# Attention before a feed-forward block: whose work the first pass's exponentials and block sums are

## The chip, the cores and the metric

The kernel runs on one core of a Trainium2 chip. The metric is the device time of one execution in microseconds (us). The core's engines work side by side, each through its own queue in order: TensorE (PE, with its weight loads PEld), VectorE (DVE), ScalarE (ACT), GpSimd (POOL) and SyncE (SP), which here only issues DMAs.

## The reference

```python
# q, k, v: (8, 8, 576, 64), float32
k_p = k.reshape(B, H, 72, 8, D).mean(axis=3)          # 72 keys: means of 8 neighbours
v_p = v.reshape(B, H, 72, 8, D).mean(axis=3)
scores = scale * np.matmul(q, k_p.transpose(0, 1, 3, 2))
scores = scores - np.max(scores, axis=-1, keepdims=True)
attn = np.exp(scores)
attn = attn / (np.sum(attn, axis=-1, keepdims=True) + 1e-09)
x = np.matmul(attn, v_p)                                # -> (4608, 512), heads side by side
gate = 1.0 / (1.0 + np.exp(-(x @ w_gate)))              # w_gate, w_val: (512, 1536)
return gate * (x @ w_val) @ w_out                       # w_out: (1536, 512)
```

## The kernel before

The 4608 rows of x are cut into nine blocks j of 512 (NB = 9, BT = 512). The weights come as 64-bit floats and are turned into float32 on the chip by bit work on ScalarE and VectorE (`to_f32`, steps "conv" and "oconv"). Each operand of a large product is split into a rounded part and a rest, so a product is three matmuls (h·h, h·l, l·h).

There are two parts. The **first pass** (`first_pass`) does attention for blocks 0, 1 and 2, converts all weights, does the whole feed-forward block for block 0 and stores it. After it, a loop of four rounds treats two blocks each with a fast scheme of seven products in place of eight (`hidden_second`, `hidden`, `second_sums`), while attention of later blocks is done piece by piece in between (`attention`).

In the first pass the steps for a block j, a pair of heads p (four pairs) and a half hf of the 512 queries are, by the names used below:

- `keys` sums eight neighbours of k on VectorE into 72 keys; `put` scales them and puts them into a block-diagonal tile `kbd` (ScalarE, two instructions of 64x72). There are five such tiles, kbd_88 to kbd_92, used in turn.
- `sc` gives the scores in PSUM: 128 queries x 4 groups x 72 keys, so 288 a row. `max` takes the negated maximum of each group of 72.
- `exps` makes the exponential. Before, it is four ScalarE instructions of 72 scores each, with the negated maximum as bias.
- `sum` adds each row's exponentials, `main` and `rest` divide by the sums, `turn` and `rturn` transpose on TensorE, `hi`/`lo` split the result, `av` multiplies by the values, `x`/`xl` split the product into the operands (tiles `xo`) of the feed-forward block.
- `vsum` and `rsum` sum eight neighbours of v for blocks 1 and 2 on VectorE (the 64 main keys, and the 8 others); block 0's are made by TensorE (`pv`).
- `mm` are the products with w_gate and w_val (tiles `chain`), `gate` and `h` join them, `acc` is the product with w_out.

In the profile the names of the first pass's scratch tiles are short: `early` is a large tile in which keys, maxima, sums and the exponentials of pairs 2 and 3 lie; `e` holds the exponentials of pairs 0 and 1; `raw`, `raws` and part of `early` are where q, k and v land.

Three tables of numbers set the order. `ORDER` lists the first pass's steps in the order in which buffers are given; it is the same in both kernels. `UNREAD` says how many matmuls whose result nobody reads are put ahead of a step (`bank_for` issues them); they are 128x128 matmuls of a constant tile. `LATER` is a permutation of all recorded instructions of the whole program, from which each engine's queue follows; semaphores between engines come from the data. All engine calls are recorded through one helper, so that nearly every row of the profile has one line, L319; tiles tell the steps apart.

Of the kernel before, what the change touches and what calls it, by code (L numbers as in the profile page):

```python
# [61 lines left out]
    "sc.0.1.1": 10, "sc.0.1.0": 1, "sc.0.0.1": 1, "sc.0.2.0": 5, "sc.0.3.1": 7, "sc.0.3.0": 2, "sc.1.0.0": 1,  # L62
    "rturn.0.1": 5, "av.0.3": 1, "mm.0.0": 1, "mm.0.1": 5, "mm.1.0": 2, "mm.1.1": 1, "mm.0.2": 1, "sc.1.1.0": 1,
# [268 lines left out]
def attention_then_ffn(ctx: ExitStack, tc: tile.TileContext, qT, kT, vm, vr, vn, sums8, wgv, wo, const, out, outT):  # L332
# [759 lines left out]
    def first_pass():  # L1092
# [79 lines left out]
        def keys(j, p):  # L1172
            k = raws["k", j, p] if j else got[f"k{p}"].rearrange("p (g t) -> p g t", t=POOL)
            nc.vector.reduce_sum(out=ks[j, p][:, :KEYS], in_=k, axis=AX.X)
# [87 lines left out]
        def v_sum(j, p):  # L1262
            pool(vs[j, p], raws["v", j, p], nc.vector)
# [199 lines left out]
```

## Time and profile before

| what | value |
|---|---|
| median of 3 runs | 934.22 us (932.6 to 936.99) |
| the profiled execution's own time | 933.27 us |
| its span, first to last instruction | 931.5 us |
| granted TensorE clock, mean | 0.999 |
| busy: PE / DVE / ACT / POOL | 918.0 / 695.0 / 572.4 / 24.1 us |
| instructions: PE / DVE / ACT / POOL | 4375 / 1062 / 1044 / 59 |
| DMA | 223.13 MB, mean 240 GB/s |

An engine's busy time says how long it had an instruction under way; matmuls overlap, so a busy PE need not run at its full pace. A fp32 matmul that is not split (scores, the unread ones) leaves two records, so 4375 records are 4159 matmuls. The views used are: the page's totals, a table of stretches of the span, the groups of like instructions, the timeline, and the chain of work that ended last.

### The profile page before, as it was taken

What the parts mean: (1) busy time and instruction counts of PE and PEld (TensorE: products, weight loads), DVE (VectorE), ACT (ScalarE), POOL (GpSimd) and SP (SyncE); (2) the same over time, 40 slices, a digit from 0 to 9 for tenths busy, and PEclk for the clock granted to TensorE, in tenths of its full rate; (3) what the DMA queues carried; (4) which work ended last, traced back from release to release, by engine and by line L of the source; (5) the groups of instructions that cost most, each with busy time, mean ns of one, the idle gap of its engine ahead of it and who ended that gap; (6) DMA issues with size and microseconds to landing.
All of it is one profiled execution on the core that took longest, in us unless ns stands there. A gap on an engine that the chain in (4) does not pass through costs nothing.

```text
span 931.5 us, 12557 instructions
## 1 busy us (share of the span) xinstructions
PE 918.0 (99%) x4375; PEld 756.0 (81%) x4375; DVE 695.0 (75%) x1062; ACT 572.4 (61%) x1044; POOL 24.1 (3%) x59
## 2 busy tenths in 40 slices
PE   8999999999999999999999999999999999999998
PEld 7778788887888878888888888888888878888886
DVE  6998888899999997976789956464768573544763
ACT  7999998679989764665575636443554353234442
POOL 1000000011121000000000000000000000000000
PEclk9999999999999999999999999999999999999999
DMA  9999496778889757787667567545456675566266
GB/s 341 372 354 346 164 392 226 254 264 304 289 303 340 265 192 262 265 301 243 210 212 235 191 223 232 191 166 186 156 193 203 216 235 191 177 198 191 94 212 192
DMA packets 90367, 223.13 MB, mean 240 GB/s; under 512 B 9536, under 2 KB 28480, under 8 KB 88768
## 3 DMA queue, kind: packets, MB, share of 16 engines
q1 hardware_dynamic: 85184, 203.97, 64.9%
q0 software_dynamic: 5120, 18.35, 5.1%
q8 instruction: 35, 0.57, 0.2%
q14 instruction: 28, 0.23, 0.1%
HBM read 168.81 MB, written 53.48 MB: 239 GB/s over the span
## 4 chain that ended last, share of the span: by engine, by line
PE 92%; ACT 5%; DMA 2%; DVE 1%; issue 0%; POOL 0%; ACTq 0%; POOLq 0%
PE chain L319 54%; PE acc L319 27%; PE sc L319 4%; PE av L319 4%; PE tp L319 2%; ACT e L319 1%; DMA parts<-keptV0C 1%; DMA oparts<-keptS 1%; ACT w L319 1%; ACT L319 1%; DMA oparts<-keptO 0%; ACT raw L319 0%; ACT y L319 0%; PE vp L319 0%; ACT parts L319 0%
## 5 line engine op out<-in xcount | busy, mean ns | idle before, releaser
L319 PE MATMUL chain<-xo,parts 128*128 128x512 f32 x2316 | 558.6, 394 | 2.9 <-ACT y L319 1.4
L319 PEld LDWEIGHTS chain<-xo,parts 128*128 128x128 f32 x2316 | 427.2, 188 | 93.4 <-ACT y L319 2.1
L319 PE MATMUL acc<-hs,oparts 128*128 128x512 f32 (+1 forms) x1011 | 235.3, 390 | 0.8 <-DMA oparts<-keptO 0.5
L319 PEld LDWEIGHTS acc<-hs,oparts 128*128 128x128 f32 x1011 | 188.2, 188 | 41.6 <-issue 1.4
L319 DVE TENSOR_TENSOR hs<-h,hs 128x1024 fp32r<-128x1024 f32 x52 | 63.3, 1221 | 37.9 <-ACT hs L319 37.5
L319 ACT CAST hs<-h 128x1024 fp32r<-128x1024 f32 x52 | 54.6, 1053 | 52.6 <-PE acc L319 51.4
L319 DVE TENSOR_TENSOR y<-chain,sG 128x512 f32<-128x512 f32 x69 | 47.2, 686 | 45.6 <-PE chain L319 32.3
L319 DVE TENSOR_TENSOR y<-chain,sV 128x512 f32<-128x512 f32 x69 | 47.2, 686 | 37.3 <-PE chain L319 25.8
L319 ACT COPY sV<-chain 128x512 f32<-128x512 f32 x69 | 40.3, 586 | 52.4 <-PE chain L319 48.6
L319 ACT COPY sG<-chain 128x512 f32<-128x512 f32 x69 | 40.4, 586 | 48.3 <-PE chain L319 47.7
L319 ACT ACTIVATE gate<-y 128x512 f32<-128x512 f32 x69 | 43.2, 631 | 39.7 <-DVE y L319 35.2
L319 ACT CAST hs<-s 128x1024 fp32r<-128x1024 f32 x36 | 37.9, 1054 | 39.8 <-PE acc L319 24.2
L319 ACT ACT_TABLE_LOAD x47 | 60.3, 1283 | 1.4 <-DVE y L319 0.5
L319 DVE TENSOR_TENSOR hs<-s,hs 128x1024 fp32r<-128x1024 f32 x36 | 44.0, 1221 | 14.6 <-ACT hs L319 14.4
L319 DVE TENSOR_TENSOR h<-y,gate 128x512 f32<-128x512 f32 x69 | 47.4, 689 | 3.8 <-ACT gate L319 1.8
L319 PE MATMUL sc<-kbd,raw 128*128 128x144 f32 (+1 forms) x260 | 41.0, 295 | 1.0 <-ACT other L319 0.7
L319 PEld LDWEIGHTS sc<-kbd,raw 128*128 128x128 f32 (+1 forms) x260 | 33.5, 177 | 9.8 <-issue 2.8
L319 PE MATMUL acc<-oparts,hs 128*128 128x512 f32 x144 | 37.8, 399 | 0.1
L319 DVE TENSOR_REDUCE m<-sc 128x4 f32<-128x288 f32 x48 | 21.7, 452 | 14.3 <-PE sc L319 14.0
L319 PEld LDWEIGHTS acc<-oparts,hs 128*128 128x128 f32 x144 | 26.3, 188 | 5.5 <-ACT pr L319 0.3
L319 DVE TENSOR_TENSOR h<-h 128x256 f32<-128x256 f32 (+2 forms) x39 | 28.3, 728 | 0.7
L319 ACT ACTIVATE gate<-chain 128x512 f32<-128x512 f32 x23 | 13.8, 599 | 18.9 <-PE chain L319 18.5
(193 smaller groups left out, 1026.0 us busy)
## 6 DMA issues: line engine op xcount, KB each, us to landing
oparts<-keptS SPq DMA_DIRECT2D x48, 512.0 KB, 4.1
oparts<-keptO SPq DMA_DIRECT2D x72, 256.0 KB, 3.5
raw<-in_wgv SPq DMA_DIRECT2D x12, 1024.0 KB, 8.7
out<-o SPq DMA_DIRECT2D x35, 256.0 KB, 4.4
raw<-in_kT SPq DMA_DIRECT2D x28, 288.0 KB, 4.8
raw<-in_qT SPq DMA_DIRECT2D x29, 256.0 KB, 4.4
raw_o<-in_wo SPq DMA_DIRECT2D x12, 512.0 KB, 6.7
keptO<-oparts SPq DMA_DIRECT2D x12, 512.0 KB, 3.8
```

Of the source, the lines that this page charges most:

```text
L319: return self._book.take(lambda: f(*args, **named))
```

## The change

`exps` becomes two instructions: VectorE adds the negated maxima to all 288 scores of a half, from PSUM into the tile of exponentials in SBUF, and ScalarE makes one exponential of the 288 in place. For blocks 1 and 2 the sums of keys and values and the scaling in `put` go to GpSimd. On GpSimd a sum is three additions, of 4, 2 and 1 columns per group (`pool`, which is there before and was given VectorE until now). Block 0's key sums stay on VectorE and its `put` on ScalarE.

```diff
 UNREAD = {
-    "sc.0.1.1": 10, "sc.0.1.0": 1, "sc.0.0.1": 1, "sc.0.2.0": 5, "sc.0.3.1": 7, "sc.0.3.0": 2, "sc.1.0.0": 1,
...
+    "sc.0.1.1": 3, "sc.0.1.0": 2, "sc.0.0.1": 5, "sc.0.0.0": 3, "sc.0.2.1": 2, "sc.0.2.0": 2, "sc.0.3.1": 2,
...
 LATER = """
-2 17 15 11 34 5 10 35 19 14 6 36 12 8 3 37 18 4 7 38 16 9 39 13 28 40 41 20 42 43 24 46 58 90 25 91 92 23 26 93 94 79
...
         def keys(j, p):
             k = raws["k", j, p] if j else got[f"k{p}"].rearrange("p (g t) -> p g t", t=POOL)
-            nc.vector.reduce_sum(out=ks[j, p][:, :KEYS], in_=k, axis=AX.X)
+            pool(ks[j, p][:, :KEYS], k, nc.gpsimd if j else nc.vector)
 
         def place_keys(j, p):
             t = kbd[slot(j, p)]
             for r, c in ((slice(0, D), slice(0, KEYS)), (slice(D, P), slice(KEYS, 2 * KEYS))):
-                nc.scalar.activation(t[r, c], ks[j, p][r, :KEYS], AF.Copy, scale=SCALE)
+                if j:
+                    nc.gpsimd.tensor_scalar(out=t[r, c], in0=ks[j, p][r, :KEYS], scalar1=SCALE, scalar2=None, op0=ALU.mult)
+                else:
+                    nc.scalar.activation(t[r, c], ks[j, p][r, :KEYS], AF.Copy, scale=SCALE)
 
         def exps(j, p, hf):
             v = scs[j, p, hf].rearrange("p i (h k) -> p (i h) k", h=2)
-            for i in range(QT):
-                k = QT * hf + i
-                nc.scalar.activation(es[p // 2][:, p % 2, k], v[:, i], AF.Exp, bias=maxima[j, p][:, k:k + 1])
+            k = slice(QT * hf, QT * hf + QT)
+            e = es[p // 2][:, p % 2, k]
+            nc.vector.tensor_tensor(
+                out=e, in0=v, in1=maxima[j, p][:, k, None].broadcast_to([P, QT, KEYS]), op=ALU.add,
+            )
+            nc.scalar.activation(e, e, AF.Exp)
...
         def v_sum(j, p):
-            pool(vs[j, p], raws["v", j, p], nc.vector)
+            pool(vs[j, p], raws["v", j, p], nc.gpsimd if j else nc.vector)
...
         def r_sum(j, g):
-            pool(vsr[j, g][:96], raws["r", j, g], nc.vector)
+            pool(vsr[j, g][:96], raws["r", j, g], nc.gpsimd if j else nc.vector)
```

`UNREAD` comes to 44 unread matmuls before and 47 now. `LATER` is another permutation from its first number to its last, so the order differs over the whole program. Three places follow. In them `early<-h` is a sum of block 0's keys, `early<-sc` with 128x4 a maximum, `zs` the row sums of exponentials, `pm` and `rest` what is divided by them, `w_235` the first weight tile under conversion.

VectorE at the start, before:

```order
L319 TENSOR_REDUCE early<-h 128x72 x2
L319 TENSOR_REDUCE early<-sc 128x4 x2
L319 TENSOR_REDUCE early<-h 128x72
L319 TENSOR_REDUCE early<-sc 128x4 x2
L319 TENSOR_REDUCE early<-h 128x72
L319 TENSOR_REDUCE early<-raw 128x64
L319 TENSOR_REDUCE early<-sc 128x4
L319 TENSOR_REDUCE zs<-e 128x16
```

VectorE at the start, now:

```order
L320 TENSOR_REDUCE early<-h 128x72 x3
L320 TENSOR_REDUCE early<-sc 128x4
L320 TENSOR_TENSOR early<-sc,early 128x288
L320 TENSOR_REDUCE early<-sc 128x4
L320 TENSOR_TENSOR early<-sc,early 128x288
L320 TENSOR_REDUCE early<-sc 128x4 x2
L320 TENSOR_TENSOR e<-sc,early 128x288
L320 TENSOR_REDUCE early<-sc 128x4
L320 TENSOR_TENSOR e<-sc,early 128x288
L320 TENSOR_REDUCE early<-sc 128x4
L320 TENSOR_TENSOR e<-sc,early 128x288 x2
L320 TENSOR_REDUCE early<-sc 128x4
```

All four key sums of block 0 (the first and a small cast stand just ahead of these rows) now come before the first maximum, and six halves have their maxima and additions before the first row sums (`zs<-e`, the next row); before, five maxima and a value sum of block 1 stood there.

GpSimd, where the clearing of tiles ends, before:

```order
L319 MEMSET vl_102 128x128
L319 MEMSET vh_95 128x128
L319 MEMSET vl_99 128x128
L319 DMA keptG4A<-parts 128x1024
L319 DMA keptG4B<-parts 128x1024
```

GpSimd in the middle of its new work, around the `put` of block 1's pair 2 into kbd_89, now:

```order
L320 TENSOR_TENSOR raw_217<-raw_217 128x72x4
L320 TENSOR_TENSOR early_200<-raw_216 128x72
L320 TENSOR_TENSOR raw_217<-raw_217 128x72x2
L320 TENSOR_TENSOR early_200<-raw_217 128x72
L320 TENSOR_TENSOR raws_210<-raws_210 96x64x2
L320 TENSOR_TENSOR early_200<-raws_210 96x64
L320 TENSOR_TENSOR raw_218<-raw_218 128x72x4
L320 TENSOR_SCALAR kbd1_89<-early_200 64x72 x2
```

Before, nothing stood between the clearing and the DMAs of the later loop; now 60 additions and 16 scalings do (20 sums and 8 `put`s). Eleven sums and the first addition of a twelfth, `keys.2.3` (raw_218), stand ahead of that `put`.

TensorE at the scores of that pair, before:

```order
L319 MATMUL chain<-xo_263,parts 128x512 x12
L319 MATMUL sc<-kbd_89,early 128x144 x2
L319 MATMUL sc<-kbd_90,early 64x144
L319 MATMUL sc<-kbd_89,early 64x144
L319 MATMUL sc<-kbd_89,early 128x144
L319 MATMUL chain<-xo_263,parts 128x512 x9
```

TensorE there, now:

```order
L320 MATMUL chain<-xo_253,parts 128x512 x3
L320 MATMUL sc<-kbd_90,early 64x144
L320 MATMUL sc<-kbd_89,early 64x144
L320 MATMUL sc<-kbd_89,early 128x144
L320 MATMUL chain<-xo_253,parts 128x512 x3
```

The scores from kbd_89 now wait for GpSimd where they waited for ScalarE, and products of the feed-forward block stand behind them in TensorE's queue in both.

More of the change, by code (lines that the diff above doesn't have):

```diff
@@ L61 @@
 UNREAD = {
-    "sc.0.1.1": 10, "sc.0.1.0": 1, "sc.0.0.1": 1, "sc.0.2.0": 5, "sc.0.3.1": 7, "sc.0.3.0": 2, "sc.1.0.0": 1,
-    "rturn.0.1": 5, "av.0.3": 1, "mm.0.0": 1, "mm.0.1": 5, "mm.1.0": 2, "mm.1.1": 1, "mm.0.2": 1, "sc.1.1.0": 1,
[4 rows of a table added]
 }
```

307 rows, old and new, of tables (LATER, UNREAD) are left out of this document.

## Prediction

> **What bounds the kernel now.** I read the page's totals and its chain first, then the stretches, then the groups and the timeline of the first 55 us.
>
> ```profile
> PE 918.0 (99%) x4375; PEld 756.0 (81%) x4375; DVE 695.0 (75%) x1062; ACT 572.4 (61%) x1044; POOL 24.1 (3%) x59
> PE 92%; ACT 5%; DMA 2%; DVE 1%; issue 0%; POOL 0%; ACTq 0%; POOLq 0%
> 767.60 101.10 PE chain L319 x444
> ```
>
> TensorE is busy for 99% of the span and carries 92% of the chain, so only what lets it run denser can shorten the kernel. Its full pace is read from the longest piece of the chain: 444 matmuls of 512 columns in 101.10 us, 0.2277 us each. I gave each matmul the usual distance from its start to the next one's, form by form (0.227 us for the 512-wide). The matmuls that are read come to 889 us of the span's 931.5; the 44 unread ones come to 10, and about 28 us is waiting. That work cannot shrink, so the most that any change here can win is some 38 us, and much of that is start-up. The stretches (us busy, count in brackets, then granted clock, DMA share and GB/s) say where it lies:
>
> ```profile
> 0.00:13.50 13.50, 10.79 (x72) 10.41 (x72) 5.63 (x12) 7.01 (x26) 2.48 (x19) 1.00 0.87 320
> 13.50:37.00 23.50, 21.40 (x128) 17.11 (x129) 22.34 (x45) 21.54 (x59) 0.00 (x0) 1.00 1.04 371
> 37.00:100.00 63.00, 61.69 (x304) 49.56 (x303) 59.73 (x99) 60.26 (x120) 0.00 (x0) 1.00 0.91 330
> 100.00:175.00 75.00, 73.88 (x363) 60.50 (x362) 61.24 (x99) 64.31 (x119) 1.74 (x3) 1.00 0.70 265
> 175.00:330.00 155.00, 153.63 (x748) 126.05 (x747) 148.76 (x258) 132.33 (x273) 19.86 (x37) 1.00 0.84 290
> 330.00:700.00 370.00, 369.99 (x1772) 305.62 (x1771) 269.09 (x415) 197.84 (x332) 0.00 (x0) 1.00 0.65 217
> 700.00:928.00 228.00, 226.62 (x1000) 186.71 (x998) 127.77 (x140) 89.02 (x120) 0.00 (x0) 1.00 0.60 192
> ```
>
> By the same account TensorE is behind its full pace (time less read work done) by 10.6 us at 13.5, 18.3 at 37, 22.1 at 69, 22.6 at 100, 26.4 at 175, 31.8 at 330, 37.1 at 700 and 38.6 at the end. So half of the loss falls in the first 37 us and 13 of the rest by 330. There VectorE (third pair of numbers) and ScalarE (fourth) are full too: 95 and 92% in the second stretch, 95 and 96% in the third, VectorE 96% in 175 to 330. After 330 neither is. The change touches the right stretch: it must be weighed by VectorE's and ScalarE's queues there, not by their sums over the span.
>
> **ScalarE, removed and added.** All rows of groups below are of the first 260 us.
>
> ```profile
> L319 ACT ACTIVATE early<-sc,early 128x72 f32<-128x72 f32 x48 | 12.4, 325 | 0.6 <-DVE early L319 0.5
> L319 ACT ACTIVATE e<-sc,early 128x72 f32<-128x72 f32 x48 | 12.3, 324 | 3.4 <-DVE early L319 3.4
> L319 ACT ACTIVATE kbd<-early 64x72 f32<-64x72 f32 x24 | 6.3, 263 | 2.5 <-DVE early L319 2.3
> L319 ACT CAST r<-rest 128x256 fp32r<-128x256 f32 x8 | 3.3, 409 | 3.1 <-DVE rest L319 3.1
> L319 ACT CAST parts<-w 128x512 fp32r<-128x512 f32 x24 | 14.7, 631 | 0.9 <-DVE w L319 0.5 <-PE chain L319 0.3
> ```
>
> 96 exponentials of 72 go: 24.7 us. 16 of the 24 `put` instructions go: 16 x 0.263 = 4.2. 24 of 288 come; no row has one, but 256 columns took 409 ns and 512 took 631, so 437 by a straight line: 10.5. ScalarE loses 18.4 us of work (17 to 19 by the two rows as ends). It is then no longer last before 175 us. I count this at nothing in the sum, since VectorE stands just as full beside it; it is the cover that lets the other terms act, and up to 4 us more if ScalarE caused the 3.8 us that TensorE falls behind between 100 and 175.
>
> **VectorE, removed and added.**
>
> ```profile
> L319 DVE TENSOR_REDUCE early<-raw 128x72 f32<-128x576 f32 x8 | 5.9, 742 | 0.0
> L319 DVE TENSOR_REDUCE early<-raws 128x64 f32<-128x512 f32 x4 | 2.7, 678 | 0.0
> L319 DVE TENSOR_REDUCE early<-raws 96x64 f32<-96x512 f32 x4 | 2.6, 672 | 0.0
> L319 DVE TENSOR_REDUCE early<-raw 128x64 f32<-128x512 f32 x3 | 2.0, 675 | 0.0
> L319 DVE TENSOR_REDUCE early<-early 128x64 f32<-128x512 f32 x1 | 0.7, 667 | 0.0
> L319 DVE TENSOR_REDUCE early<-sc 128x4 f32<-128x288 f32 x24 | 10.6, 451 | 4.8 <-PE sc L319 4.7
> L319 DVE TENSOR_TENSOR h<-h 128x256 f32<-128x256 f32 x16 | 6.8, 422 | 0.4
> L319 DVE TENSOR_TENSOR h<-h 128x512 f32<-128x512 f32 x8 | 5.5, 685 | 0.1
> ```
>
> The 20 sums of blocks 1 and 2 go: 5.9 + 2.7 + 2.6 + 2.0 + 0.7 = 13.9 us. 24 additions of 288 come, at 455 ns between the 422 and 685 of 256 and 512 columns, which is what a maximum over the same 288 takes (451): 10.9. **First term: -3.0 us** (ends -3.8 at 422 and 0 at 580).
>
> The second term is VectorE's idle time at the start:
>
> ```profile
> 3.45 1.53 DVE L319 TENSOR_REDUCE early<-h 128x72 f32<-128x576 f32 x2 [2.58 <-DMA h<-in_kT]
> 8.48 0.95 DVE L319 TENSOR_REDUCE early<-sc 128x4 f32<-128x288 f32 x2 [3.50 <-PE sc L319]
> 12.73 0.46 DVE L319 TENSOR_REDUCE early<-sc 128x4 f32<-128x288 f32 x1 [0.63 <-PE sc L319]
> 13.48 1.35 DVE L319 TENSOR_REDUCE zs<-e 128x16 f32<-128x1152 f32 x1 [0.29 <-ACT e L319]
> ```
>
> Up to the first row sums at 13.48 it waits 7.0 us in four waits, and has done 5.6 us of work. Now the four key sums (3.0 us) come first; the last one's keys are the seventh of the DMAs, 1.8 MB, there near 7 us at the 371 GB/s of the second stretch and a start of 2. They end near 8. From there each half brings a maximum and an addition, 0.9 us, while TensorE gives a half in 0.6, so VectorE waits no more; six additions and seven maxima later the row sums start at about 13.3, with 8.3 us done. **Second term: -2.9 us** (ends 0 and -3.5: the waits of 3.50 + 0.63 + 0.29 less what the later landing adds).
>
> **GpSimd** takes 60 additions and 16 scalings. Nothing in the trace adds on GpSimd; the nearest rows are its clearings:
>
> ```profile
> L319 POOL MEMSET kbd<- 128x144 f32 x5 | 1.0, 221 | 0.3 <-POOLq L1454 0.3
> L319 POOL MEMSET vh<- 128x128 f32 x5 | 1.0, 205 | 0.0
> L1454 POOL MEMSET const-float32-0.0<- 128x1 f32 x1 | 0.1, 98 | 0.2 <-issue 0.2
> ```
>
> That is 0.10 us and 0.85 ns a column: 0.34 + 0.22 + 0.16 = 0.72 us a sum, 14.5 for all, and 2.6 for the scalings: 17 us as the lower end. An addition reads twice what a clearing writes; three times, 51 us, is my upper end. I take twice, 34 us (the clearing's rate, once for each operand). It hides as long as it comes before its reader. The tightest place is `put` 1.2 for the scores here:
>
> ```profile
> 53.90 1.47 PE L319 MATMUL sc<-kbd,early 128*128 128x144 f32 x9
> ```
>
> Ahead of it stand eleven sums and one addition; the twelfth's keys are the 48th DMA, 16.5 MB into the queue. By 37 us 13.0 MB are there (13.5 x 320 + 23.5 x 371 kB), and at 330 to 371 GB/s the rest takes 9.3 to 10.5: 46 to 48 us. The scores now stand 2.3 us of work earlier in TensorE's queue than at 53.90, and run at 50 to 52. So GpSimd has some 3 us to spare, and its own work (eleven sums of 1.4 in the 30 us since the first values landed) fits. Taken at nothing.
>
> **Three more unread matmuls**, 0.22 us each: they stand where TensorE waits, but I charge 0.7 (ends 0 and 0.7). The DMAs are the same; the order past 330 us differs, and I count that at 0 (ends -2 and +2, half of what TensorE falls behind from 330 to 700).
>
> **The sum**: -3.0 - 2.9 + 0.7 = -5.2 on the profiled execution's 933.27 (span 931.5 and 1.8 around it), 928.1. The median of the runs is 0.95 above that execution, so 929.0 us.
>
> **Rivals.** (1) *It stays within 0.5%, because VectorE's queue keeps the deadline.* TensorE's first products need the splits of x, the last of which is here:
>
> ```profile
> 36.55 1.28 DVE L319 TENSOR_TENSOR xo<-av,xo 128x512 fp32r<-128x512 f32 x2
> ```
>
> Ahead of the second one stood 27.9 us of VectorE's work by the groups' durations, and now 29.4: eight additions came in, two sums went out. With 2.9 us less idle time that is only 1.4 us earlier; the sums it is spared lie later, when VectorE is 96% busy in 175 to 330 with work that waits for TensorE's results. Then the gain is 1.4 and the time 933. For it: that stretch is full. Against it: between 37 and 100 VectorE is spared most sums, and TensorE lost 4.3 us there.
>
> (2) *Slower: GpSimd's additions hold up VectorE.* If the two block each other while both read SBUF, VectorE loses GpSimd's time in the share of its own that is open to it. Its costliest such rows from 13.5 to 100 us:
>
> ```profile
> L319 DVE TENSOR_TENSOR parts<-w,parts 128x512 fp32r<-128x512 f32 x17 | 11.5, 683 | 0.1
> L319 DVE SCALAR_TENSOR_TENSOR w<-w,raw 128x1024 uint32<-128x1024 uint32 x9 | 11.0, 1219 | 0.7 <-ACT raw L319 0.6
> L319 DVE TENSOR_SCALAR w<-w 128x1024 f32<-128x1024 f32 x9 | 6.2, 684 | 0.6 <-ACT w L319 0.6
> ```
>
> With the smaller groups such instructions take some 50 of VectorE's 82 us there, 0.6. At 17 us of GpSimd that is 10 us lost, at 34 us 20. About half would be had back, since TensorE falls 9.2 us further behind from 100 to 330 now, in waits that a later TensorE finds shorter. So 934.2 - 5.2 + 5 to + 10, up to 939; beyond 10 us of loss after this recovery it is slower by over 0.5%. For it: in the first pass nothing else gives VectorE room. Against it: no row shows it; GpSimd only issued DMAs beside VectorE. [...]
>
> (3) *GpSimd's keys come late.* If a sum takes over 3 us, eleven pass the 50 us at which TensorE reaches pair 2's scores; at 4 us a sum TensorE stands some 10 us with products behind, about 936 after what the others gain meanwhile.
>
> **Chances.** The forecast 0.44; rival 1 0.38; rival 2 0.14; rival 3 0.04. The forecast alone reaches from 924.5 (ScalarE's 4 us added) to 931. The range, 924.5 to 938, takes in rival 1 and most of rival 2, and leaves out the upper end of 2 and the far ends of 1. 0.5% is 4.7 us, about what a measurement tells from no change (the three runs spread over 4.4). From the forecast 0.41 falls to faster, from rivals 1 and 2 0.02; nearly all of rival 1 and a part of the others is the same; slower has the rest of 2 and 3, 0.15.
>
> **What the profile would show.** ScalarE's first stretches no longer full and VectorE's sum 3 us lower; the first row sums near 13.3 us with 8 us of work done; TensorE behind by about 19 us at 69 us where it is 22 now, and by 26 at 330. I am wrong if two-input VectorE rows are longer than their 683 and 1219 ns (rival 2), if the row of scores from kbd names GpSimd as the one waited for (3), or if TensorE is as far behind at 330 us as before (1).

## The result, and the profile after

The changed kernel takes 943.72 us (median of 6 runs, 942.17 to 944.10), the kernel before, beside it, 934.45 (6 runs). The ratio is 1.0093, with a 95% interval of 1.0079 to 1.0106: slower by 8.7 us, where I forecast 5 us less and gave slower 15 in 100. The profiled execution took 944.10, with a span of 942.1. The page's totals and the engines of its chain:

```profile
PE 924.1 (98%) x4381; PEld 760.8 (81%) x4381; DVE 700.0 (74%) x1066; ACT 558.8 (59%) x956; POOL 73.4 (8%) x135
PE 81%; DVE 7%; ACT 4%; DMA 3%; issue 1%; POOL 0%; SPq 0%; DVEq 0%; ACTq 0%; POOLq 0%
```

TensorE carried 92% of the chain before and carries 81% now; VectorE has 7% where it had 1. The same stretches as before (us busy and count of PE, PEld, DVE, ACT, POOL, then granted clock, DMA share, GB/s):

```profile
0.00:13.50 13.50, 12.06 (x76) 11.75 (x77) 6.93 (x16) 5.07 (x14) 2.51 (x19) 1.00 0.87 292
13.50:37.00 23.50, 19.21 (x109) 15.81 (x108) 19.85 (x38) 16.44 (x32) 13.20 (x23) 0.85 1.03 378
37.00:100.00 63.00, 59.95 (x287) 47.12 (x287) 57.63 (x92) 52.87 (x82) 35.24 (x52) 1.00 0.82 305
100.00:175.00 75.00, 74.46 (x369) 61.44 (x368) 66.93 (x107) 61.57 (x99) 2.06 (x4) 1.00 0.76 277
175.00:330.00 155.00, 152.36 (x748) 124.74 (x747) 142.66 (x257) 130.93 (x275) 20.37 (x38) 1.00 0.81 283
330.00:700.00 370.00, 367.76 (x1747) 303.33 (x1746) 266.63 (x408) 196.71 (x330) 0.00 (x0) 1.00 0.67 216
```

ScalarE is no longer full (53 of 63 us where it had 60). In the second stretch TensorE has 19 matmul records fewer, and its granted clock is 0.85 where it was 1.00. GpSimd is busy for 13 and 35 us in two stretches in which it did nothing. Now VectorE's groups from 13.5 to 100 us (count, busy, mean ns). The first four stood at 683, 1219, 684 and 450 ns before; the fifth, one half of the new additions, is new:

```profile
L320 DVE TENSOR_TENSOR parts<-w,parts 128x512 fp32r<-128x512 f32 x16 | 12.3, 781 | 0.6 <-ACT parts L320 0.3 <-DMA raw<-in_kT 0.2
L320 DVE SCALAR_TENSOR_TENSOR w<-w,raw 128x1024 uint32<-128x1024 uint32 x8 | 9.9, 1243 | 0.1
L320 DVE TENSOR_SCALAR w<-w 128x1024 f32<-128x1024 f32 x8 | 7.0, 882 | 0.0
L320 DVE TENSOR_REDUCE early<-sc 128x4 f32<-128x288 f32 x14 | 6.1, 449 | 1.3 <-PE sc L320 1.1
L320 DVE TENSOR_TENSOR e<-sc,early 128x288 f32<-128x288 f32 x8 | 3.4, 447 | 0.1
```

Subtractions with two inputs in SBUF take 98 ns more, clippings of weights (`w<-w`; before, 1024 columns in 684 ns where a subtraction took 683 for 512, the "double-rate" rows of two expectations below) 198 more. The merges of weights (`w<-w,raw`) have two inputs in SBUF as well and take only 24 more. The maxima (449 ns, before 450) and the new additions, which take one input from PSUM (447 ns, in E11 449), are not longer. Against the median of the same kind of row before, VectorE's rows up to 130 us are longer by 6.9 us in sum, 2.2 of it before 37 us. Here is how it looks from close by, two of VectorE's rows first, then GpSimd's at that time:

```profile
34.73 1.24 DVE L320 TENSOR_TENSOR parts<-w,parts 128x512 fp32r<-128x512 f32 x1
36.00 0.69 DVE L320 TENSOR_TENSOR pl<-tp,ph 128x512 fp32r<-128x512 f32 x1
34.69 1.53 POOL L320 TENSOR_TENSOR raws<-raws 96x256 f32<-96x256 f32 x2
```

The subtraction that GpSimd's additions overlap takes 1.24 us; the next of the same size, with a PSUM input, takes 0.69.

TensorE's lag behind full pace (time less the read work done, as in the prediction) tells where the time went. Each column is one execution. The price of a matmul differs a little from the prediction's (before is 30.3 us behind at 330 here and 31.8 there), so compare the columns with one another only. The kernels of the other columns come below.

| lag at, us | before | after | E3 | E8 | E11 | E13 | E15 | E16 |
|---|---|---|---|---|---|---|---|---|
| 13.5 | 10.6 | 9.7 | 10.1 | 9.7 | 10.1 | 10.1 | 10.1 | 10.8 |
| 37 | 18.2 | 22.6 | 23.1 | 20.1 | 19.6 | 21.0 | 21.4 | 22.8 |
| 100 | 22.3 | 30.0 | 33.9 | 28.2 | 22.6 | 24.8 | 28.9 | 26.8 |
| 330 | 30.3 | 38.0 | 42.0 | 36.1 | 30.2 | 36.6 | 37.3 | 36.6 |
| 500 | 32.3 | 44.2 | 45.3 | 40.3 | 33.7 | 39.2 | 40.3 | 39.0 |
| 900 | 34.4 | 45.1 | 46.9 | 41.5 | 35.6 | 41.3 | 41.7 | 41.5 |

After loses 5.3 us more than before between 13.5 and 37, 3.3 more up to 100, nothing up to 330, and 4.2 more between 330 and 500. E13's column is that of the slowest of its 12 runs, 940.62 us, 5 us above their median; it loses 4 us between 100 and 330 that the others, but for E16's 2, don't lose.

### The profile page after: what moved, and what is told of

Read it like the earlier page. It is cut to its first block, busy times and chain, and to the rows that moved or that the text cites. A ratio compares the mean times of both kernels' runs of the same rounds, so it can differ in the third digit from the quotient of the medians.

```text
span 942.1 us, 12552 instructions
## 1 busy us (share of the span) xinstructions
PE 924.1 (98%) x4381; PEld 760.8 (81%) x4381; DVE 700.0 (74%) x1066; ACT 558.8 (59%) x956; POOL 73.4 (8%) x135
## 4 chain that ended last, share of the span: by engine, by line
PE 81%; DVE 7%; ACT 4%; DMA 3%; issue 1%; POOL 0%; SPq 0%; DVEq 0%; ACTq 0%; POOLq 0%
PE chain L320 47%; PE acc L320 27%; PE av L320 3%; PE sc L320 3%; PE tp L320 2%; DMA raw<-in_vr 1%; ACT L320 1%; DVE w L320 1%; DMA raw<-in_wgv 1%; DMA keptG5C<-sums 1%; DVE parts L320 1%; DVE zs L320 1%; DVE early L320 1%; ACT e L320 1%; ACT parts L320 1%
## 5 line engine op out<-in xcount | busy, mean ns | idle before, releaser
L320 PE MATMUL acc<-hs,oparts 128*128 128x512 f32 x1011 | 234.3, 390 | 0.1
L320 DVE TENSOR_TENSOR y<-chain,sG 128x512 f32<-128x512 f32 x69 | 47.2, 687 | 37.3 <-PE chain L320 17.5
L320 DVE TENSOR_TENSOR hs<-s,hs 128x1024 fp32r<-128x1024 f32 x36 | 43.7, 1219 | 4.8 <-ACT hs L320 4.4
L320 PEld LDWEIGHTS sc<-kbd,raw 128*128 128x128 f32 (+1 forms) x260 | 33.7, 178 | 9.4 <-issue 3.5
L320 ACT COPY xs<-av 128x512 f32<-128x512 f32 x32 | 18.7, 583 | 16.0 <-PE av L320 15.5
```

The lines of the kernel that those rows point to most:

```text
L320: return self._book.take(lambda: f(*args, **named))
```

## The experiments

The change is three things: edits of the exponentials, edits of the sums, and another order. For an experiment with "the order of" one kernel, each instruction of the other code was put where its counterpart stands: one addition for the first of four exponentials, three additions for one sum. All ratios are to the kernel before, with 95% intervals; 0.001 is 0.93 us.

**E1 to E4: the edits and the order apart.** E1 has the new code in the old order:

```diff
-UNREAD, LATER of after
+UNREAD, LATER of before, with exps and sums in the place of their counterparts
```

> All edits of the change (additions on VectorE and one exponential, sums and scalings of blocks 1 and 2 on GpSimd), but every instruction stands where the kernel before had its counterpart, with the unread matmuls of before. Theory A, GpSimd's additions hold up VectorE: VectorE's rows with two SBUF inputs are stretched as in the changed kernel (parts<-w,parts over 750 ns against 682, some 7 us in all), about 936 to 942 us. Theory B, the new order of the queues costs the time and the edits are harmless: the rows may be stretched, but 927 to 932 us, below the 934 of before.

E2 is the reverse, the old code in the new order:

```diff
-UNREAD, LATER of before
+UNREAD, LATER of after, with exps and sums in the place of their counterparts
```

> The code of before (four exponentials of 72, all sums on VectorE, scalings on ScalarE), every instruction where the changed kernel has its counterpart. Theory A: nothing reads on GpSimd, so VectorE's rows have their lengths of before, but VectorE has the 13.9 us of sums again: 934 to 940 us. Theory B: the order is what costs: 943 us or more, the early stall of TensorE at 22 to 26 us is still there.

E3 is the changed kernel with

```diff
-            pool(vs[j, p], raws["v", j, p], nc.gpsimd if j else nc.vector)
+            pool(vs[j, p], raws["v", j, p], nc.vector)
```

and `keys`, `r_sum` and `put` treated alike:

> The changed kernel with the sums of blocks 1 and 2 back on VectorE and the scalings back on ScalarE, each in the place that it has in the changed kernel; the exponentials stay changed. Theory A: VectorE's rows are back at 682 and 684 ns, which saves 7 us and costs 13.9 us of sums that are partly hidden: 938 to 945 us. Theory B: the order still costs, and VectorE has more to do: 945 to 952 us.

E4 is the kernel before with the reverse of this edit, in its own order:

> The kernel before with its own order and exponentials; only the 20 sums and 8 pairs of scalings of blocks 1 and 2 go to GpSimd, in place. Theory A: VectorE loses 13.9 us of sums and its two-input rows grow by about 7 us, and sums that take 2 us in place of 0.7 are late for their readers: 933 to 940 us. Theory B: nothing of the order is changed, so VectorE's room is a gain: 926 to 932 us.

Measured: E1 945.64 us, 1.0115 (1.0092 to 1.0138). E2 955.92, 1.0226 (1.0204 to 1.0249). E3 947.77, 1.0144 (1.0118 to 1.0169). E4 937.92, 1.0032 (1.0018 to 1.0047). So the order is no cause by itself: the new code is slower in the old order too (E1's interval overlaps that of the changed kernel), and theory B, which wanted E1 below the kernel before, falls. The old code is slowest of all in the new order, 21 us above its own. But theory A does not carry it alone either: in the new order the sums on GpSimd gain 4.8 us over E3, though they lengthen VectorE's rows. In E4, where the rows grew by 9.6 us by the measure above, the time rose by only 3.0. That the rows grow is GpSimd's doing; E3's rows from 13.5 to 100 us, with the same order and nothing read on GpSimd:

```profile
L313 DVE TENSOR_TENSOR parts<-w,parts 128x512 fp32r<-128x512 f32 x16 | 10.7, 683 | 0.4 <-ACT parts L313 0.3
```

**E5, E6: the exponentials alone, and the sums alone in the new order.** E5 is the kernel before with the diff's edit of `exps`:

> The kernel before in its own order; only the exponentials are changed (one addition of 288 on VectorE where the first of the four exponentials stood, one exponential of 288 where the last stood). Nothing adds on GpSimd. Theory A, contention with GpSimd is what costs: ScalarE has 14 us less, VectorE 10.9 us more in unstretched rows, 932 to 938 us. Theory C, the additions on VectorE cost by themselves, since VectorE's queue decides the start and each addition there delays the splits of x and the weights: 940 to 945 us, VectorE's rows at 683 ns all the same.

E6 is the changed kernel with

```diff
-            nc.vector.tensor_tensor(out=e, in0=v, in1=maxima[...].broadcast_to([P, QT, KEYS]), op=ALU.add)
-            nc.scalar.activation(e, e, AF.Exp)
+            for i in range(QT):
+                nc.scalar.activation(es[...], v[:, i], AF.Exp, bias=maxima[...])
```

> The changed kernel with the exponentials of before (four of 72 on ScalarE, standing where the addition stands), the sums on GpSimd as changed, in the changed order. If the two edits add up, this is the time of the old code in the new order less the 4 us that the sums on GpSimd gained there: 950 to 954 us. Theory C, VectorE's additions cost: with 10.9 us less on VectorE it would fall below the changed kernel's 943.7, to 936 to 942 us. If the new order was built around the new exponentials, it is slower than the changed kernel by 6 us or more.

E5 took 938.83, 1.0049 (1.0032 to 1.0067): 10.9 us more on VectorE cost 4.6 us, between the two ranges and nearer to theory C's sign, although ScalarE had 14 us less to do. E6 took 952.39, 1.0177 (1.0161 to 1.0193). That is the first expected case, in which the two edits add up: in the new order the sums gain 4.6 us with the old exponentials (E2 to E6) and 4.8 with the new ones. The third case, that the new order needs the new exponentials, holds too (8.7 us slower than the changed kernel); theory C's does not. In the old order the edits add up badly: 1.0049 and 1.0032 alone, 1.0115 together, 3 us more than the sum, which is about what the intervals can tell.

**E7: GpSimd's reads alone.** In the kernel before, each sum stays on VectorE, and behind it

```diff
+            for k in (4, 2, 1):
+                xk = x.broadcast_to([n, k, c])          # x: the sum just made
+                nc.gpsimd.tensor_tensor(out=scratch[:n, :k, :c], in0=xk, in1=xk, op=ALU.add)
```

> The kernel before in its own order with all its work as before. Behind each of VectorE's 20 sums of blocks 1 and 2 GpSimd makes three additions of 4, 2 and 1 times 72 (or 64) columns on a scratch tile that nobody reads: GpSimd's reads alone, with nothing taken from VectorE and nobody waiting for GpSimd. Theory A: VectorE's rows with two SBUF inputs and its double-rate rows are stretched by 5 to 8 us in all, and the time is 937 to 942 us. Rival: the stretch is swallowed by waits, 934 to 936 us.

936.80, 1.0017 (1.0005 to 1.0029). Reads that serve nobody cost 1.6 us. The time lies between the two expectations, and the growth of VectorE's rows was missed: 3.6 us, not 5 to 8. Only 6 of the 60 additions started before 37 us, where the changed kernel has 19.

**E8: the granted clock.** The clock of the second stretch falls, to 0.50 from 23.90 to 30.72 us, where TensorE waits for the rests of the attention weights (tile `r`). E8 puts eight more unread matmuls there:

```diff
-    "rturn.0.0": 2,
+    "rturn.0.0": 10,
```

Two windows of after, then the same of E8:

```profile
22.00:26.00 4.00, 1.58 (x9) 1.45 (x10) 3.31 (x10) 3.26 (x9) 3.15 (x6) 0.74 1.05 391
26.00:30.00 4.00, 4.00 (x17) 3.62 (x16) 2.12 (x3) 1.61 (x3) 2.52 (x5) 0.50 1.01 367
```

```profile
22.00:26.00 4.00, 2.71 (x24) 2.43 (x23) 3.41 (x10) 3.26 (x10) 2.11 (x5) 1.00 1.05 389
26.00:30.00 4.00, 3.78 (x28) 3.09 (x26) 3.89 (x7) 3.72 (x5) 3.61 (x7) 1.00 1.01 367
```

> The changed kernel with eight more unread matmuls just ahead of the first transposes of the rests, where TensorE stands idle from 21.4 to 23.6 us. Theory D, the idle stretch drops the granted clock (0.74 in 22 to 26 us, 0.50 in 26 to 30 us), and that costs: the clock stays at 1.00 there, TensorE gains about 2 us, 941 to 942.5 us. Rival: between 25 and 50 us TensorE waits for VectorE's splits of x anyway, and the lower clock only fills waits: 943 to 944.5 us.

940.95, 1.0067 (1.0046 to 1.0087), at the lower end of theory D's range; the interval just overlaps that of after, and by the ratios 2.4 us come back. The first timeline is of after, the second of E8:

```profile
23.65 0.50 PE L320 MATMUL tr<-identr,r 128*96 128x128 f32 x4 [2.25 <-DVE r L320]
24.93 1.62 PE L320 MATMUL av<-cst 128*128 128x128 f32 x6 [0.77 <-DVE early L320]
26.34 1.49 PE L320 MATMUL tp<-cst 128*128 128x128 f32 x6
27.48 0.77 PE L320 MATMUL av<-ph,vh 128*128 128x512 f32 x1
```

```profile
21.13 1.95 PE L315 MATMUL tr<-cst 128*128 128x128 f32 x16
24.82 0.91 PE L315 MATMUL av<-cst 128*128 128x128 f32 x6 [0.83 <-DVE early L315]
25.56 0.83 PE L315 MATMUL tp<-cst 128*128 128x128 f32 x6
26.15 0.48 PE L315 MATMUL av<-ph,vh 128*128 128x512 f32 x1
```

At half clock the six unread matmuls (operand `cst`, twelve records) ahead of the first product with the values take 2.5 us instead of 1.3, and hold up the product by 1.3. The fall is not the doing of GpSimd's reads alone: E3, where GpSimd adds nothing, has it too, for 3.4 us instead of 6.8. In before, E1 and E4, which have the old order, the clock stays at 1.00 from 13.5 to 37 us. E3's window:

```profile
26.00:30.00 4.00, 4.00 (x22) 3.64 (x20) 3.32 (x5) 2.64 (x6) 0.00 (x0) 0.65 1.01 359
```

**E9, E10: which additions on VectorE cost.** As E5, but in `exps` the old form is kept under `if j == 0:` (E9) or `if j:` (E10).

> The kernel before in its own order; the exponentials are changed for blocks 1 and 2 only (16 additions on VectorE, 7.2 us, from some 40 us on), block 0 keeps its 32 exponentials of 72; all sums stay. Theory C (VectorE's additions cost where they stand ahead of the splits that TensorE's first products wait for, that is for block 0): 933 to 936 us, as before. Rival E (an addition on VectorE costs wherever VectorE is full, until 175 us): two thirds of the 4.6 us that all 24 cost, 937 to 939 us.

> The kernel before in its own order; the exponentials are changed for block 0 only (eight additions, 3.6 us, ahead of the splits of x). Theory C: nearly the whole price of the additions, 937 to 940 us, with TensorE some 1.4 us further behind at 37 us than before. Rival E: a third of it, 936 us or less.

E9 took 938.07, 1.0038 (1.0022 to 1.0053), E10 936.79, 1.0016 (0.9998 to 1.0035). Theory C, that only the additions ahead of the first splits count, falls: the 16 later ones cost 3.6 us and the eight early ones 1.5 (not told apart from none), in proportion to their number, as rival E said.

**E11: GpSimd's additions cut.** In the changed kernel, `pool` makes the last addition only:

```diff
-        while n > 1:
+        while n > 1 and False:
```

> The changed kernel in which GpSimd makes only the last of the three additions of each sum (20 of 60; the sums of blocks 1 and 2 are then of two of the eight neighbours). GpSimd's time from 13.5 to 100 us falls from 46 us to about 18. Theory A (contention and late keys from GpSimd are a main cost): most of the 7 us by which VectorE's rows were stretched is back, 939 to 941 us. Rival F (the order and the early idle stretch cost, GpSimd little): 942.5 to 944 us, as the changed kernel.

934.80, 0.9997 (0.9983 to 1.0010). All that the changed kernel had lost is back, 9 us, more than theory A had expected. VectorE's rows are longer by 0.9 us in sum instead of 6.9, and the clock stays at 1.00. But GpSimd is also busy for less time and its sums come earlier; E13 and E14 take these apart.

**E12: the order of the later loop.** From the instruction that TensorE reaches at 200 us on, E12 follows the order of before. The place that it is about is the stall in the chain of after, where a load of values behind a store decides:

```profile
390.00 7.47 DMA keptG5C<-sums
397.49 3.77 DMA raw<-in_vr
401.28 0.69 DVE s L320
401.97 0.61 DVE pl L320
402.63 2.13 PE av L320 x8
```

> The changed kernel; what stands behind the instruction that TensorE reaches at 200 us follows the order of before, on all engines. Theory G (the changed kernel's own order of the later loop makes the stall at 402.6 us, where VectorE waits for a value load and TensorE falls 4.5 us further behind between 400 and 450): that is gone, 938.5 to 941 us, and TensorE at 600 us is no more than 8 us further behind than before. Rival H (the stall follows from the delay that TensorE brings along from the first 55 us, not from the order): 943 to 945 us.

942.77, 1.0080 (1.0055 to 1.0104), not told apart from after: rival H by the time. By the trace theory G isn't refuted: in E12 the lag grew by 5.2 us between 200 and 250 (after 0.4) and by 4.2 between 330 and 400 (after 0.6) in places of its own. With after's order, E11 has no DMA in its chain from 395 to 445 us and loses 3.5 us between 330 and 500, E3 has the same load in its chain and loses 3.3, after 6.2. A part of the difference is the clock: ahead of the last row above TensorE waited 1.94 us, and in after the clock was then at half from 402.8 to 406.2 us, about 1.7 us of work; E3 and E11 have no such fall between 330 and 500 (1.00 in both). What makes the rest stays open.

**E13, E14: what of GpSimd's additions costs.** E13 is the changed kernel with

```diff
-            eng.tensor_tensor(out=raw[:, :, :n], in0=raw[:, :, :n], in1=raw[:, :, n:2 * n], op=ALU.add)
+            eng.memset(raw[:, :, :2 * n], 0.0)
```

> The changed kernel in which the two wide additions of each sum on GpSimd are replaced by clearings of 576 and of 288 columns (about 0.59 and 0.34 us by the trace's 0.10 us and 0.85 ns a column); the last addition stays, and its sum is zero. GpSimd writes SBUF for as long, but reads nothing in those instructions. Theory A (reads of GpSimd and VectorE's two-input or double-rate rows exclude each other): VectorE's rows near 685 ns, 934 to 938 us. Rival L (what costs is that GpSimd is busy and its sums come late): 941 to 944 us, as the changed kernel.

E14 moves the line of the last addition ahead of the loop:

> The changed kernel with the three additions of each sum in turned order: the last one, which gives the sum (of two of eight neighbours), first, then the two wide ones, whose results nobody reads. GpSimd reads as much as in the changed kernel, but each sum is there 1.3 us earlier. Theory A: 942 to 945 us. Rival L: 936 to 940 us.

E13 took 935.53, 1.0011 (0.9994 to 1.0029). GpSimd is busy for 26.6 us between 37 and 100, against 35.2 in after and 12.1 in E11, and the 7.7 us are gone: what costs here is that GpSimd reads. VectorE's rows grew by 1.6 us in sum. Two of them from 13.5 to 100 us, E13's first, then E11's clipping:

```profile
L315 DVE TENSOR_TENSOR parts<-w,parts 128x512 fp32r<-128x512 f32 x16 | 10.8, 688 | 0.6 <-ACT parts L315 0.3 <-DMA raw<-in_kT 0.2
L315 DVE TENSOR_SCALAR w<-w 128x1024 f32<-128x1024 f32 x9 | 7.0, 791 | 0.0
L313 DVE TENSOR_SCALAR w<-w 128x1024 f32<-128x1024 f32 x9 | 6.5, 727 | 0.0
```

The subtraction takes 688 ns beside clearings, where it had 781 beside additions and 685 in E11; the clipping takes 791, where it had 882 and 727. The merges of weights, with two SBUF inputs, stayed near their length also beside GpSimd's additions (1243 ns in after, 1241 in E13, 1219 before).

E14 took 939.71, 1.0053 (1.0032 to 1.0075), between the two theories. Its clock was 1.00 from 22 to 30 us, and it was 2.5 us less behind at 37 than after; from 37 to 100 it lost 7.4 us, the same as after. So an earlier sum won nothing there, and rival L has nothing left to explain there. All that E14's lag gains on the changed kernel's up to 330 us, it gains before 37 us, where its clock held; why it held there and not in after is not shown.

**E15, E16: where they cost.** Both have

```diff
-        n = POOL // 2
+        n = 1 if cut else POOL // 2        # cut: (kind, j, p) in SOON (E15), not in SOON (E16)
```

> The changed kernel; the seven sums whose additions run before some 39 us (values 1.1, 2.3 and 1.0, keys 1.0, 1.1 and 1.2, the rest of values 1.0) are cut to their last addition, the other 13 are whole. Theory A1 (the additions cost where VectorE's chain to the splits of x sets TensorE's start): nearly all of the 8.9 us is back, 935 to 937 us, with the clock at 1.00 from 22 to 30 us. A2 (they cost in proportion to their number, until 95 us): a third, 940 to 942 us.

> The reverse: the seven early sums whole, the 13 later ones cut to their last addition. A1: 941 to 943.5 us, nearly the changed kernel's time. A2: two thirds are back, 937 to 939 us.

E15 took 940.69, 1.0067 (1.0040 to 1.0093), E16 939.41, 1.0047 (1.0027 to 1.0066): 2.4 and 4.3 us back of 9.0. Theory A1 falls: E15 has little back, and its clock fell too (0.66 from 26 to 30 us). A2 fits better, though E16's median is 0.4 us above its range, and the two gains make 6.7 of the 9.0, a gap that the intervals can't tell from none. The table of lags agrees: from 37 to 100 us after, E8 and E15, with the late additions whole, lose 7.4, 8.1 and 7.5 us; E11, E13 and E16, without them, 3.0, 3.8 and 4.0; before, 4.1. So GpSimd's additions cost TensorE about 4 us there, where VectorE's rows were lengthened by 4.7.

No version here beat the kernel before.

## Why the prediction was wrong, step by step

In the new order the ratios make a sum: the old code 21.1 us above before, the new exponentials -7.7 (E2 to E3), the sums taken off VectorE and the scalings off ScalarE, without the reads of GpSimd's wide additions, -12.4 (E3 to E13), those reads +7.7 (E13 to after). The first three come to +1 us (E13), the fourth makes the result.

So two steps of the sum failed. The one that turned the sign is GpSimd, "taken at nothing": its reads cost 7.7 us. The other is the gain of 5.2 us, of which nothing came: without the reads the time is 1 us above before, not told apart from it.

- **Where the time is lost** (the lag, the stretches up to 100 us): right; all that the changed kernel lost against the kernel before up to 330 us was lost there.
- **ScalarE, counted at nothing**: the price was right, 443 ns for an exponential of 288 where I took 437, and ScalarE was no longer full. E5 shows that this room was worth less than what VectorE paid for it.
- **First term, VectorE -3.0 us**: the netting of sums over the span failed. An addition took 447 ns, as priced (455). But 10.9 us of additions cost 4.6 us in the old order (E5), and the sums taken away were worth 12.4 us in the new order without the reads of GpSimd's wide additions, while with them, in the old order, they cost 3.0 (E4). One microsecond on VectorE is worth what its place and the order make of it; the difference of two such sums said little.
- **Second term, -2.9 us of idle time**: mis-sized. The row sums started at 15.36 us, not 13.3, with the 8.3 us of work done that I had forecast. VectorE had stood idle for 7.1 us up to there and for 7.9 before: 0.8 won. A part was my own adding up: six times 0.9 and one maximum behind 8 us give 13.9. For the rest, the last three key sums started only here:

```profile
6.72 0.75 DVE L320 TENSOR_REDUCE early<-h 128x72 f32<-128x576 f32 x1 [2.19 <-DMA h<-in_kT]
8.17 1.47 DVE L320 TENSOR_REDUCE early<-h 128x72 f32<-128x576 f32 x2 [0.69 <-DMA h<-in_kT]
```

  I had them end near 8 us at the 371 GB/s of a later stretch; the first 13.5 us moved 292 GB/s, and they ended at 9.64. The last split of x started at 42.97, not earlier than 37.15: VectorE had been busy for 32.8 us ahead of it (28.1 before; 2.2 of the difference is that rows were longer) and idle for 10.2 (9.0).
- **GpSimd at nothing**: this step sank the prediction. Its work was hidden in the sense that I meant: additions and scalings took some 50 us, near my upper end of 51, and TensorE waited for GpSimd's keys for 0.6 us from 13 to 110 us (0.2 and 0.4, with its weight loads), so rival 3 did not come. But I looked only for who waits for a result, and so missed whose instructions grew beside its reads (the subtractions from 683 to 781 ns, the clippings from 684 to 882).
- **Three more unread matmuls, +0.7**: the count was no issue, their place was. With eight more at one wait the clock held and 2.4 us came back (E8).
- **Order past 330 us, 0**: the profiled execution lost 4.2 us more than before between 330 and 500. Kernels with the same later order lost 0.4 to 2.2 more there (E3, E8, E11, E13, E15, E16, one execution each). Of after's 4.2, about 1.7 is the clock's fall at 402.8 us; the rest stays open (E12).
- **What the profile should have shown**: ScalarE's stretches, yes. VectorE's sum is not 3 us lower but 5.0 higher, which is -3.0 and the 6.9 by which rows were longer and about 1 more; the lag is 27.4 us at 69 us and 38.0 at 330, where I had written 19 and 26. The longer two-input rows were named as rival 2's sign.
- **Rival 1** (VectorE keeps its deadline, within 0.5%) gives the time of the change without GpSimd's wide additions: E11 and E13. Its reason doesn't fit: the last split of x started at 38.5 us in E11 and 40.8 in E13, not 1.4 us ahead of the 37.15 of before.
- **Rival 2** was right that VectorE's rows grow beside GpSimd's additions. Its sizes were off both ways. That the rows it counts, 0.6 of VectorE's time, would lose all of GpSimd's time beside them was my estimate, and no run shows it: of the three that it lists, subtractions grew by 98 ns, clippings by 198 and merges by 24. VectorE lost 6.9 us, not 10 to 20: for some 20 of GpSimd's 49 us the row of VectorE beside it was a reduction or had a PSUM input, and such rows did not grow (maxima 449 ns where 450, `pl<-tp,ph` 684 where 680). Of the 6.9 nothing was had back, where I had taken half. The longer rows stood in the queue that TensorE's first products wait for. Added to a gain of 5.2 that was not there, my 5 to 10 gave 939 as the upper end; 1 us lost and 7.7 on top of it make the 8.7 measured.

## What to carry to other kernels

Work given to an idle engine need not be free: here GpSimd's reads cost 7.7 us, though TensorE waited for GpSimd's keys for only 0.6. Before moving elementwise work to GpSimd, list the VectorE instructions that will run beside it, and compare their lengths before and after: here subtractions with two SBUF inputs went from 683 to 781 ns and clippings from 684 to 882, while maxima stayed at 449 and merges went from 1219 to 1243. Test with clearings in place of the additions, which keep most of GpSimd's time (here 26.6 of 35.2 us) and drop its reads. Don't net one engine's added and removed microseconds over a span; ask for each which wait it stands in. And where TensorE's waits grow, look at its granted clock in windows of 4 us before anything else (here 0.74 and 0.50 from 22 to 30 us, in a stretch with a mean of 0.85).

## What the runs showed of the hardware that I had not expected

- GpSimd's rows vary too: in the changed kernel the last addition of a rest of values, 64 columns of 96 partitions, took 0.30 us at its shortest (36.30 us) and 1.67 at its longest. The longest ran beside a merge of weights with two SBUF inputs that took 1.21, as before (1219 ns). GpSimd's row, then VectorE's:

```profile
47.35 1.67 POOL L320 TENSOR_TENSOR early<-raws 96x64 f32<-96x64 f32 x1
47.65 1.21 DVE L320 SCALAR_TENSOR_TENSOR w<-w,raw 128x1024 uint32<-128x1024 uint32 x1
```

- Beside clearings on GpSimd (E13) VectorE's clippings of weights took 791 ns where E11, without them, had 727, and its subtractions 688 where E11 had 685.
- The granted clock fell to 0.50 at 23.9 us in after, behind a gap of 2.25 us in TensorE's rows. In E14 it stayed at 1.00 from 22 to 30 us, with TensorE busy for 1.74 of the 4 us from 22 to 26, where after had 1.58. In after the clock changed at 23.90, 30.72, 402.78, 406.19 and 942.08 us; the stretches between these are 6.83, 372.05, 3.41 and 535.89 us, whole multiples of 3.413. Cut into pieces of that length at these points, TensorE was busy for 34, 43 and 0% of the three pieces that ended in a fall, and for 58% or more of every other piece from 3.4 us on. Before has one fall, at 930.21 us, behind a piece that was busy for 26%; no other piece from 1.8 us on was below 52%.
